# Grouped-query decode on one core: 8 MB tiles in three buffers, keys transposed in place, scores held in PSUM

## Chip, cores and metric

One core of a Trainium2 chip runs the kernel. The metric is device time in microseconds (us), the median of several executions. The engines are named as in the profile: PE (TensorE matmul), PEld (its weight load), DVE (VectorE), ACT (ScalarE), POOL (GpSimd) and SP (SyncE, which here only issues loads). "SPq" and "ACTq" are the queues from which SP and ACT issue DMAs; the transfers themselves run on 16 DMA engines.

## The reference

One query position attends to 65,536 keys. There are 32 query heads and 8 key/value heads, so four query heads share one key/value head (a group). All inputs are bf16.

```python
B, Hq, Hkv, Sq, Sk, D = 1, 32, 8, 1, 65536, 128
k = jnp.repeat(k, Hq // Hkv, axis=1)
v = jnp.repeat(v, Hq // Hkv, axis=1)
scores = jnp.einsum("bhqd,bhkd->bhqk", q, k) * D ** -0.5
p = softmax(scores, axis=-1)
return jnp.einsum("bhqk,bhkd->bhqd", p, v)
```

Keys and values are 134 MB each, and each is read once: 268.44 MB in all.

## The kernel before

A group's keys are laid out as 128 partitions of 512 rows (a row is 128 bf16 numbers, 256 B). They are loaded as four tiles of 128 rows a partition: 32 KB a partition, 4 MB a tile, one DMA each on SP's queue. Values are loaded in the same way. Keys and values share one pool of four such buffers (`iopool`, tag `io`).

The loop runs over g = 0 to 8 and s = 0 to 3. In each step it loads and uses key tile s of group g, and then value tile s of group g-1. So values run one group behind keys, and the last pass has values alone. Within that, a scheduler orders the instructions of an engine by their dependences; the loads on SP's queue go out in order, and each waits until its buffer is free.

A key tile goes through `k_step`. DVE transposes the tile, seen as 4-byte words, in 32x32 blocks into small buffers `T` (line 135, four instructions of 128x2048 words a tile). PE then multiplies each `T` with the group's queries, which lie spread out with zeros around them in `wq` (line 144, 32 matmuls of 512 columns a tile, all accumulating into one PSUM bank `sc`). ACT copies the bank to `S_g` in SBUF (line 151). There are two query buffers, `wq0` and `wq1`; POOL fills the one for the next group (line 109).

After four key tiles `softmax` takes the maximum over `S_g` (line 156), spreads the per-head maximum over the partitions with two small PE instructions (lines 160 and 172), and ends in `nmb` (line 174), the negated scaled maximum. ACT makes `E_g = exp(...)` in one instruction and sums it into `lsum_all` (line 177). `transpose_weights` transposes `E_g` into `ET` (line 190).

A value tile goes through `v_stream`: 32 matmuls with `ET` as weights (line 213), accumulating over the group into `psum_o`. `pick` takes the wanted blocks out of `psum_o` (lines 224 and 230), and `finish` divides by the sums and stores (lines 237 to 250). The last value tile is loaded in pieces of 64, 32, 16, 8, 4 and 4 rows, and `finish_last` treats its late rows one by one, so that little is left to do when the last piece lands.

At the start the queries come by four small transfers on ACT's queue (line 70), each a copy of all heads to 32 partitions, while SP already issues the first key loads.

Of the kernel before, what the change touches and what calls it, by code (L numbers as in the profile page):

```python
# [13 lines left out]
NT = 128  # L14
NW = 16
# [5 lines left out]
def kernel(  # L21
# [26 lines left out]
    W = NT // NW  # L48
    assert W * HPG == 32 and KT == 4
# [6 lines left out]
    iopool = ctx.enter_context(tc.tile_pool(name="iopool", bufs=4))  # L56
    tpool = ctx.enter_context(tc.tile_pool(name="tpool", bufs=3))
    spool = ctx.enter_context(tc.tile_pool(name="spool", bufs=2))
    epool = ctx.enter_context(tc.tile_pool(name="epool", bufs=2))
    opool = ctx.enter_context(tc.tile_pool(name="opool", bufs=2))  # L60
    stats = ctx.enter_context(tc.tile_pool(name="stats", bufs=2))
    psc = ctx.enter_context(tc.tile_pool(name="psc", bufs=3, space=bass.MemoryType.PSUM))
    psm = ctx.enter_context(tc.tile_pool(name="psm", bufs=1, space=bass.MemoryType.PSUM))
    psf = ctx.enter_context(tc.tile_pool(name="psf", bufs=1, space=bass.MemoryType.PSUM))
# [3 lines left out]
    qn = const.tile([P, D], bf16)  # L68
# [5 lines left out]
    Wq = []  # L74
    for x in range(2):
        wq = const.tile([P, 4 * WX], bf16, name=f"wq{x}")
        nc.vector.memset(wq[:, :], 0.0)
        Wq.append(wq)
# [17 lines left out]
    lsum_all = const.tile([P, Hkv], fp32)  # L96
    o_all = const.tile([P, Hkv, D], fp32)

# [5 lines left out]
    def queries(g):  # L104
        eng = nc.vector if g == 0 else nc.gpsimd
        wv = Wq[g % 2][:, :].rearrange("p (b r x) -> p b r x", b=2, r=2)
        for a in range(4):
            qd = slice(32 * a, 32 * a + 32)
            eng.tensor_copy(  # L109
                out=wv[qd, :, :, 32 * a + 28:32 * a + 28 + HPG],  # L110
                in_=qv[qd, :, :, g * HPG:(g + 1) * HPG],
            )
# [3 lines left out]
    S_tiles, E_tiles, ET_tiles, o_tiles = {}, {}, {}, {}  # L116

    def k_load(g, s):
        kn = iopool.tile([P, NT, D], bf16, name="kn", tag="io", align_bytes=2048)
        src = k[0, g].rearrange("(p n) d -> p n d", p=P)  # L120
        nc.sync.dma_start(out=kn[:, :, :], in_=src[:, s * NT:(s + 1) * NT, :])
        return kn

    def k_step(g, s, kn):
        if s == 0:
            S_tiles[g] = spool.tile([P, KT, 4 * P], fp32, name="S_g")
        wq = Wq[g % 2]
        kv = kn[:, :, :].rearrange("p (c w) d -> p w c d", w=W)
        sc = psc.tile([P, 4 * P], fp32, name="sc")
        for w in range(W):  # L130
            if s == 0 and w == W // 2 and g > 0:
                transpose_weights(g - 1)
            if w % 2 == 0:
                T = tpool.tile([P, 2, NW, D], bf16, name="T")
                nc.vector.transpose(  # L135
                    out=T[:, :, :, :].bitcast(fp32),
                    in_=kv[:, w:w + 2].bitcast(fp32),
                )
            Tv = T[:, w % 2].rearrange("p n (b i r) -> p n b i r", b=2, r=2)
            for b in range(2):  # L140
                for r in range(2):
                    bp = 2 * b + r
                    at = bp * WX + 28 - 4 * w
                    nc.tensor.matmul(  # L144
                        out=sc[:, :],
                        lhsT=wq[:, at:at + P],
                        rhs=Tv[:, :, b, :, r],
                        start=(w == 0 and bp == 0),
                        stop=(w == W - 1 and bp == 3),
                    )  # L150
        nc.scalar.copy(out=S_tiles[g][:, s, :], in_=sc[:, :])  # L151

    def softmax(g):
        S_g = S_tiles[g]
        mx = stats.tile([P, 1], fp32, name="mx")
        nc.vector.tensor_reduce(  # L156
            out=mx[:, :], in_=S_g[:, :, :].rearrange("p n c -> p (n c)"), axis=AX.X, op=ALU.max
        )
# [6 lines left out]
        mrow = stats.tile([1, P], fp32, name="mrow")  # L165
# [10 lines left out]
        E_g = epool.tile([P, KT, 4 * P], bf16, name="E_g")  # L176
        nc.scalar.activation(  # L177
            out=E_g[:, :, :].rearrange("p s x -> p (s x)"),
            in_=S_g[:, :, :].rearrange("p s x -> p (s x)"),
            func=ACT.Exp,  # L180
            bias=nmb[:, 0:1],
            scale=SCALE,
            accum_out=lsum_all[:, g:g + 1],
        )
        E_tiles[g] = E_g

    def transpose_weights(g):

        ET = epool.tile([P, KT, NW, 32], bf16, name="ET")
        nc.vector.transpose(  # L190
            out=ET[:, :, :, :].rearrange("p s c x -> p (s c x)"),
            in_=E_tiles[g][:, :, :].rearrange("p s x -> p (s x)"),
        )
        ET_tiles[g] = ET

    def v_load(g, s, pieces=(NT,)):
        vb = iopool.tile([P, NT, D], bf16, name="vb", tag="io", align_bytes=2048)
        src = v[0, g].rearrange("(p n) d -> p n d", p=P)
        x = 0
        for step in pieces:  # L200
            n0 = s * NT + x
            nc.sync.dma_start(out=vb[:, x:x + step, :], in_=src[:, n0:n0 + step, :])  # L202
            x += step
        return vb

    def v_stream(g, s, vb, rows, last):

        if s == 0:
            o_tiles[g] = pso.tile([P, 4, D], fp32, name="psum_o")
        for c in range(rows // W):  # L210
            for x in range(2):
                j = 2 * x + c % 2
                nc.tensor.matmul(  # L213
                    out=o_tiles[g][32 * j:32 * j + 32, :, :],
                    lhsT=ET_tiles[g][:, s, c, :],
                    rhs=vb[:, c * W + 4 * x:c * W + 4 * x + 4, :],
                    start=(s == 0 and c < 2),
                    stop=(last and c >= rows // W - 2),
                )

    def pick(g):

        o_m = opool.tile([P, 4, D], fp32, name="o_m")
        nc.vector.tensor_tensor(  # L224
            out=o_m[:, :, :],
            in0=o_tiles[g][:, :, :],
            in1=mask[:, :].unsqueeze(2).broadcast_to([P, 4, D]),
            op=ALU.mult,
        )
        nc.vector.tensor_reduce(  # L230
            out=o_all[:, g, :], in_=o_m[:, :, :].rearrange("p x d -> p d x"), axis=AX.X, op=ALU.add
        )

    def sums(g0, n):

        psum_l = psm.tile([HPG, n], fp32, name="psum_l", tag="misc")
        nc.tensor.matmul(out=psum_l[:, :], lhsT=sel[:, :], rhs=lsum_all[:, g0:g0 + n], start=True, stop=True)  # L237
        rl = stats.tile([HPG, n], fp32, name="rl")
        nc.vector.reciprocal(out=rl[:, :], in_=psum_l[:, :])
        return rl  # L240

    def store(g0, n, psum_f, rl):
        o_out = stats.tile([HPG, n, D], bf16, name="o_out")
        nc.vector.tensor_tensor(  # L244
            out=o_out[:, :, :],
# [3 lines left out]
        )  # L249
        nc.scalar.dma_start(  # L250
            out=out[0, :, 0, :].rearrange("(g h) d -> h g d", h=HPG)[:, g0:g0 + n, :], in_=o_out[:, :, :]
        )

    def finish(g0, n):
        rl = sums(g0, n)
        psum_f = psf.tile([HPG, n, D], fp32, name="psum_f", tag="fin")
        nc.tensor.matmul(  # L257
            out=psum_f[:, :, :], lhsT=sel[:, :], rhs=o_all[:, g0:g0 + n, :], start=True, stop=True
        )
        store(g0, n, psum_f, rl)  # L260

    def finish_last(g, s, vb):
# [6 lines left out]
        v_stream(g, s, vb, n1, True)  # L269
        pick(g)  # L270
        psum_oT = pso.tile([P, HPG], fp32, name="psum_oT", tag="psum_o")
        psum_f = psf.tile([HPG, 1, D], fp32, name="psum_f", tag="fin")

        def w4(n):
            c, w = divmod(n, W)
            return ET[:, s, c, HPG * w:HPG * w + HPG]

        def single(a, b):
            for n in range(a, b):
                nc.tensor.matmul(  # L280
                    out=psum_f[:, 0, :], lhsT=w4(n), rhs=vb[:, n, :], start=False, stop=(n == NT - 1)
                )

        with tc.manual_schedule(engines={mybir.EngineType.PE}):
            for n in range(n1, n2):
                if n == n1 + 32:
                    nc.tensor.matmul(  # L287
                        out=psum_f[:, 0, :], lhsT=sel[:, :], rhs=o_all[:, g, :], start=True, stop=False
                    )
                nc.tensor.matmul(  # L290
                    out=psum_oT[:, :], lhsT=vb[:, n, :], rhs=w4(n), start=(n == n1), stop=(n == n2 - 1)
# [4 lines left out]
            psum_t2 = psm.tile([HPG, D], fp32, name="psum_t2", tag="misc")  # L296
            nc.tensor.transpose(out=psum_t2[:, :], in_=oT[:, :], identity=ident[:, :])
            single(n3, NT)
        o_t = stats.tile([HPG, D], fp32, name="o_t")
        nc.vector.tensor_scalar_mul(out=o_t[:, :], in0=psum_t2[:, :], scalar1=rl[:, 0:1])  # L300
        o_last = stats.tile([HPG, D], bf16, name="o_last")
        nc.vector.scalar_tensor_tensor(  # L302
            out=o_last[:, :], in0=psum_f[:, 0, :], scalar=rl[:, 0:1], in1=o_t[:, :], op0=ALU.mult, op1=ALU.add
        )
        nc.scalar.dma_start(out=out[0, g * HPG:(g + 1) * HPG, 0, :], in_=o_last[:, :])

    for g in range(Hkv + 1):
        if 0 < g < Hkv:
            queries(g)
        for s in range(KT):  # L310
            if g < Hkv:
                k_step(g, s, k_load(g, s))
            elif s == 0:
                transpose_weights(g - 1)
# [44 lines left out]
```

## Time and profile before

| what | value |
|---|---|
| median of 3 runs | 632.07 us (631.75 to 632.32) |
| the profiled execution | 631.69 us |
| its span, first to last instruction | 629.6 us |
| granted TensorE clock, mean | 0.78 |
| busy: PE, DVE, ACT, POOL | 363.2, 340.4, 36.8, 6.4 us |
| loads on SP's queue | 69 DMAs, 268.44 MB |
| HBM rate over the span | 426 GB/s |
| SP's first load issued | 0.74 us after the span's start |

Times on the page are of one profiled execution, which is why its own time stands beside the span: 2.1 us lie outside the span. Busy time of an engine is a share of the whole span; whether it matters depends on what the others wait for. In the rows of groups, the numbers behind the bar are busy us, mean ns of one instruction, and the engine's idle time just before them with what ended it. In the rows of waits they are us in total, how many, and the longest.

### The profile page before, as it was taken

The page shows a single profiled execution, that of the slowest core. Times are in us where ns is not written, and L with a number is a line of the kernel's source. Part 1 is how long each engine was busy: PE and PEld are TensorE (multiplying, and loading weights), DVE is VectorE, ACT ScalarE, POOL GpSimd, SP SyncE. Part 2 cuts the span into 40 slices and gives each one's busy share as a digit, 9 for nine tenths or more (in the row PEclk, how much of TensorE's full clock was granted, in tenths as well). Part 3 has the DMA queues.
Part 4 walks back from the last instruction along what each step waited for, and adds up shares of the span by engine and source line. Part 5 has one row for each costly group of instructions (what it writes and reads, how often), then busy time and mean ns, then how long its engine had stood idle before and what let it go on. Part 6 is the DMA issues. An engine that isn't in the chain of part 4 may idle for free.

```text
span 629.6 us, 4872 instructions
## 1 busy us (share of the span) xinstructions
PE 363.2 (58%) x2133; PEld 141.5 (22%) x2133; DVE 340.4 (54%) x201; ACT 36.8 (6%) x49; POOL 6.4 (1%) x37
## 2 busy tenths in 40 slices
PE   0686836745557554575645856447665466644645
PEld 0232312211222221222211222112221122211212
DVE  0998833774337753377543775436754366553511
ACT  0000100010000100001000010001000010000100
POOL 0000000000000000000000000000000000000000
PEclk9998988767887677876778867788677787767856
DMA  8999999999999999999999999999999999999996
GB/s 369 433 434 431 433 432 434 432 433 433 432 433 432 433 433 432 433 432 433 432 433 433 430 434 434 433 432 433 435 432 433 432 433 433 432 433 434 431 430 267
DMA packets 10192, 268.78 MB, mean 427 GB/s; under 512 B 1340, under 2 KB 1596, under 8 KB 1852
## 3 DMA queue, kind: packets, MB, share of 16 engines
q1 hardware_dynamic: 9936, 268.44, 99.0%
q8 instruction: 16, 0.26, 0.1%
q10 hardware_dynamic: 236, 0.04, 0.0%
q14 instruction: 4, 0.03, 0.0%
HBM read 268.47 MB, written 0.01 MB: 426 GB/s over the span
## 4 chain that ended last, share of the span: by engine, by line
DMA 73%; DVE 12%; issue 11%; PE 2%; ACTq 0%; DVEq 0%; SPq 0%
DMA kn<-in_k_dram 66%; DVE T L135 12%; DMA vb<-in_v_dram 5%; DMA qn<-in_q_dram 2%; PE sc L144 2%; PE psum_o L213 0%; PE psum_oT L290 0%; ACTq L70 0%; PE psum_f L280 0%; DVEq L135 0%; DVE wq L109 0%; PE psum_f L287 0%; DVE sel L83 0%; DVE o_last L302 0%; SPq L202 0%
## 5 line engine op out<-in xcount | busy, mean ns | idle before, releaser
L144 PE MATMUL sc<-T,wq 128*128 128x512 bf16 x1024 | 287.9, 445 | 220.2 <-DVE T L135 220.2
L135 DVE STREAM_TRANSPOSE T<-kn 128x2048 f32<-128x2048 f32 x128 | 284.2, 2277 | 198.6 <-DMA kn<-in_k_dram 198.6
L144 PEld LDWEIGHTS <-wq 128*128 128x128 bf16 x1024 | 109.5, 109 | 394.6 <-issue 159.5
L213 PE MATMUL psum_o<-vb,ET 128*32 128x512 bf16 x1008 | 65.1, 403 | 12.0 <-DMA vb<-in_v_dram 9.8
L151 ACT COPY S_g<-sc 128x512 f32<-128x512 f32 x32 | 18.8, 587 | 510.8 <-PE sc L144 510.8
L213 PEld LDWEIGHTS <-ET 128*32 128x32 bf16 x1008 | 25.5, 100 | 49.2 <-issue 28.3
L156 DVE TENSOR_REDUCE mx<-S_g 128x1 f32<-128x2048 f32 x8 | 18.3, 2286 | 26.1 <-ACT S_g L151 26.1
L190 DVE STREAM_TRANSPOSE ET<-E_g 128x2048 bf16<-128x2048 bf16 x8 | 18.5, 2311 | 16.3 <-ACT E_g L177 16.3
L177 ACT ACTIVATE E_g<-S_g,nmb 128x2048 bf16<-128x2048 f32 x8 | 16.0, 2001 | 47.6 <-DVE nmb L174 40.4
L224 DVE TENSOR_TENSOR o_m<-psum_o,mask 128x512 f32<-128x512 f32 x8 | 5.5, 682 | 21.5 <-PE psum_o L213 21.5
L109 POOL COPY wq<-qx 32x16 bf16<-32x16 bf16 x28 | 5.3, 190 | 426.9 <-PE sc L144 410.2
L160 PE MATMUL psum_t<-ident,mx 128*1 128x128 f32 x8 | 2.2, 270 | 11.2 <-DVE mx L156 11.2
L100 DVE STREAM_TRANSPOSE qx<-qn 128x64 f32<-128x64 f32 x1 | 0.2, 245 | 15.0 <-DMA qn<-in_q_dram 15.0
L172 PE MATMUL psum_b<-one,mrow 1*128 1x1 f32 x16 | 3.5, 288 | 8.3 <-DVE mrow L166 8.3
L230 DVE TENSOR_REDUCE o_all<-o_m 128x128 f32<-128x512 f32 x8 | 8.0, 1000 | 0.0
L172 PEld LDWEIGHTS psum_b<-one,mrow 1*128 1x128 f32 x16 | 3.0, 232 | 12.2 <-issue 11.4
L237 PE MATMUL psum_l<-lsum_all,sel 128*4 128x4 f32 (+2 forms) x6 | 0.6, 166 | 7.7 <-ACT E_g L177 7.7
L257 PE MATMUL psum_f<-o_all,sel 128*4 128x512 f32 (+1 forms) x4 | 2.6, 730 | 2.9 <-DVE o_all L230 2.9
L160 PEld LDWEIGHTS psum_t<-ident,mx 128*1 128x1 f32 x8 | 0.6, 79 | 15.1 <-DVE mx L156 11.6
L174 DVE COPY nmb<-psum_b 128x1 f32<-128x1 f32 x8 | 1.2, 152 | 2.9 <-PE psum_b L172 2.9
L290 PE MATMUL psum_oT<-ET,vb 128*128 128x4 bf16 x56 | 1.8, 167 | 1.4 <-DMA vb<-in_v_dram 1.4
L244 DVE TENSOR_TENSOR o_out<-psum_f,rl 4x512 bf16<-4x512 f32 (+1 forms) x2 | 1.2, 612 | 2.5 <-PE psum_f L257 2.5
(30 smaller groups left out, 16.1 us busy)
## 6 DMA issues: line engine op xcount, KB each, us to landing
kn<-in_k_dram SPq DMA_DIRECT2D x32, 4096.0 KB, 29.6
vb<-in_v_dram SPq DMA_DIRECT2D x31, 4096.0 KB, 34.1
vb<-in_v_dram SPq DMA_DIRECT2D x1, 2048.0 KB, 29.5
vb<-in_v_dram SPq DMA_DIRECT2D x1, 1024.0 KB, 31.6
vb<-in_v_dram SPq DMA_DIRECT2D x1, 512.0 KB, 32.3
vb<-in_v_dram SPq DMA_DIRECT2D x1, 256.0 KB, 32.5
vb<-in_v_dram SPq DMA_DIRECT2D x2, 128.0 KB
qn<-in_q_dram ACTq DMA_DIRECT2D x4, 8.0 KB, 10.1
```

Of the source, the lines that this page charges most:

```text
L109: eng.tensor_copy(out=wv[qd, :, :, 32 * a + 28:32 * a + 28 + HPG], in_=qv[qd, :, :, g * HPG:(g + 1) * HPG],)
L135: nc.vector.transpose(out=T[:, :, :, :].bitcast(fp32), in_=kv[:, w:w + 2].bitcast(fp32),)
L144: nc.tensor.matmul(out=sc[:, :], lhsT=wq[:, at:at + P], rhs=Tv[:, :, b, :, r], start=(w == 0 and bp == 0), stop=(w == W - 1 and bp == 3),)
L151: nc.scalar.copy(out=S_tiles[g][:, s, :], in_=sc[:, :])
L156: nc.vector.tensor_reduce(out=mx[:, :], in_=S_g[:, :, :].rearrange("p n c -> p (n c)"), axis=AX.X, op=ALU.max)
L160: nc.tensor.transpose(out=psum_t[:, :], in_=mx[:, :], identity=ident[:, :])
L172: nc.tensor.matmul(out=psum_b[:, :], lhsT=mrow[:, :], rhs=one[:, :], start=True, stop=True)
L177: nc.scalar.activation(out=E_g[:, :, :].rearrange("p s x -> p (s x)"), in_=S_g[:, :, :].rearrange("p s x -> p (s x)"), func=ACT.Exp, bias= ...
L190: nc.vector.transpose(out=ET[:, :, :, :].rearrange("p s c x -> p (s c x)"), in_=E_tiles[g][:, :, :].rearrange("p s x -> p (s x)"),)
L213: nc.tensor.matmul(out=o_tiles[g][32 * j:32 * j + 32, :, :], lhsT=ET_tiles[g][:, s, c, :], rhs=vb[:, c * W + 4 * x:c * W + 4 * x + 4, :], ...
L224: nc.vector.tensor_tensor(out=o_m[:, :, :], in0=o_tiles[g][:, :, :], in1=mask[:, :].unsqueeze(2).broadcast_to([P, 4, D]), op=ALU.mult,)
L230: nc.vector.tensor_reduce(out=o_all[:, g, :], in_=o_m[:, :, :].rearrange("p x d -> p d x"), axis=AX.X, op=ALU.add)
```

## The change

- `NT` goes from 128 to 256 rows a partition: tiles are 64 KB a partition, 8 MB, two a group for keys and two for values. `iopool` has three buffers instead of four. A tile is worked through in halves of `NB` = 128 rows (`U` = 2 halves a tile, `NU` = 4 a group), and each half has its own PSUM bank `sc`.
- Keys are transposed in place: DVE writes the transposed words back over the tile, 128x4096 words an instruction, four a tile, and PE reads the tile itself. `T` goes. Which 16 rows go into one matmul changes with it: they are now next to each other.
- Scores stay in PSUM until the exp. The copy to `S_g` goes; DVE takes a maximum over each half's bank, and ACT makes four exps a group, one from each bank. There are five `sc` banks instead of three.
- `E_g`, `ET`, the query buffer `wq` and the statistics are single buffers. The query tile `qn` borrows the place of `E_g`. `ET` is made at the end of `softmax`.
- `pick` becomes four instructions that multiply and add, `finish` runs for two groups at a time, and results collect in `o_out`.
- Loads have one function, `load`. The first key tile comes in four pieces of 64 rows; the last value tile in pieces of 128, 64, 32, 16, 8, 4 and 4. Queries still come by four transfers.

```diff
-NT = 128
+NT = 256
+NB = 128
...
-    iopool = ctx.enter_context(tc.tile_pool(name="iopool", bufs=4))
-    tpool = ctx.enter_context(tc.tile_pool(name="tpool", bufs=3))
-    epool = ctx.enter_context(tc.tile_pool(name="epool", bufs=2))
-    psc = ctx.enter_context(tc.tile_pool(name="psc", bufs=3, space=bass.MemoryType.PSUM))
+    iopool = ctx.enter_context(tc.tile_pool(name="iopool", bufs=3))
+    epool = ctx.enter_context(tc.tile_pool(name="epool", bufs=1))
+    psc = ctx.enter_context(tc.tile_pool(name="psc", bufs=5, space=bass.MemoryType.PSUM))
...
+    def load(x, name, g, s, pieces=(NT,)):
+        t = iopool.tile([P, NT, D], bf16, name=name, tag="io", align_bytes=2048)
+        src = x[0, g].rearrange("(p n) d -> p n d", p=P)
+        n = 0
+        for step in pieces:
+            n0 = s * NT + n
+            nc.sync.dma_start(out=t[:, n:n + step, :], in_=src[:, n0:n0 + step, :])
+            n += step
+        return t
...
     def k_step(g, s, kn):
...
-            if w % 2 == 0:
-                T = tpool.tile([P, 2, NW, D], bf16, name="T")
-                nc.vector.transpose(
-                    out=T[:, :, :, :].bitcast(fp32),
-                    in_=kv[:, w:w + 2].bitcast(fp32),
-                )
...
-        nc.scalar.copy(out=S_tiles[g][:, s, :], in_=sc[:, :])
+        for u in range(U):
+            nu = s * U + u
+            sc = psc.tile([P, 4 * P], fp32, name="sc")
+            sc_tiles[g, nu] = sc
+            for w in range(W):
+                n0 = u * NB + w * NW
+                if w % 4 == 0:
+                    groups = kn[:, n0:n0 + 4 * NW, :].rearrange("p n d -> p (n d)").bitcast(fp32)
+                    nc.vector.transpose(out=groups, in_=groups)
+                kv = kn[:, n0:n0 + NW, :].rearrange("p n (b i r) -> p n b i r", b=2, r=2)
...
+            nc.vector.tensor_reduce(out=mx_tiles[g][:, nu:nu + 1], in_=sc[:, :], axis=AX.X, op=ALU.max)
...
+        for nu in range(NU):
+            nc.scalar.activation(
+                out=E_g[:, nu, :],
+                in_=sc_tiles[g, nu][:, :],
+                func=ACT.Exp,
+                bias=nmb[:, 0:1],
+                scale=SCALE,
+                accum_out=lsum_all[:, g, nu:nu + 1],
+            )
...
     def v_stream(g, s, vb, halves, last):
...
+        for u in range(U):
+            vv = vb[:, u * NB:(u + 1) * NB, :].rearrange("p (w c) d -> p w c d", c=NW)
+            n = min(2, halves - 2 * u)
+            for x in range(n):
+                for c in range(NW):
+                    j = 2 * x + c % 2
+                    nc.tensor.matmul(
+                        out=o_tiles[g][32 * j:32 * j + 32, :, :],
+                        lhsT=ET_tiles[g][:, s * U + u, c, :],
+                        rhs=vv[:, 4 * x:4 * x + 4, c, :],
...
     def pick(g):
...
+        nc.vector.tensor_scalar_mul(out=o, in0=o_tiles[g][:, 0, :], scalar1=mask[:, 0:1])
+        for x in range(1, 4):
+            nc.vector.scalar_tensor_tensor(
+                out=o, in0=o_tiles[g][:, x, :], scalar=mask[:, x:x + 1], in1=o, op0=ALU.mult, op1=ALU.add
+            )
...
-                k_step(g, s, k_load(g, s))
+                pieces = (64,) * 4 if g == 0 and s == 0 else (NT,)
+                k_step(g, s, load(k, "kn", g, s, pieces))
```

## The prediction

> **What bounds the kernel now.** I read the page's header and DMA rows first, then the queue's table, the groups by cost, the chain of waits, the waits of the SP queue and the timeline at both ends.
>
> ```profile
> span 629.6 us, 4872 instructions
> PE 363.2 (58%) x2133; PEld 141.5 (22%) x2133; DVE 340.4 (54%) x201; ACT 36.8 (6%) x49; POOL 6.4 (1%) x37
> ...
> DMA  8999999999999999999999999999999999999996
> GB/s 369 433 434 431 433 432 434 432 433 433 432 433 432 433 433 432 433 432 433 432 433 433 430 434 434 433 432 433 435 432 433 432 433 433 432 433 434 431 430 267
> ...
> q1 hardware_dynamic: 9936, 268.44, 99.0%
> ```
>
> No compute engine is above 58%, while the one queue that carries keys and values fills 99.0% of what 16 engines have, at 430 to 435 GB/s in every slice but the first and the last. There is no dip at a group's end or anywhere else, so nothing that the compute engines do holds a load up. The packet records of the trace say the same: the first data packet starts at 1.75 us, the last ends at 625.51 us, and all packets of q1 last together 623.24 us an engine. Of the 623.76 us between them the engines lack 0.5 us. So the span is 1.75 us, then the loads, then 4.1 us of tail.
>
> ```profile
> SPq L121 <- DVE T L135: 273.7, 28, 14.2
> ...
> SPq L202 <- PE psum_o L213: 108.4, 28, 5.0
> ```
>
> SP does wait for buffers: a key buffer comes free when DVE has transposed it out, a value buffer when PE has read it. These waits cost nothing, because a load lands 29.6 us (keys) or 34.1 us (values) after its issue, which is three transfers of 9.7 us: two are still queued ahead at the issue. The chain of waits has the same shape all along:
>
> ```profile
> 72.41 2.07 issue
> 74.62 2.06 issue
> 76.67 4.47 DVE T L135 x2
> 81.16 29.74 DMA kn<-in_k_dram
> ```
>
> Its DMA pieces are three transfers long, so a third of each is time spent behind other loads. I take from it only who frees the buffer.
>
> **What a packet costs.** The packet records (median ns) are 46 for 1,024 B, 84 for 2,048, 159 for 4,096, 309 for 8,192, 611 for 16,384, and 1,213 for 32,768, of which there are 8,064; a 4-byte completion write takes 9 and there are 1,104. These lie on one line: from 16,384 to 32,768 B it is 602 ns, so 32,768 B cost 1,204 ns of bytes and about 9 ns that belong to the packet. One engine's sum before: 504 packets of 1,213, 8 x (611+309+159+84+46+46) for the last tile's pieces, 69 completions of 9, together 622.0 us. The trace's 623.24 has 1.2 us more; about 0.6 us of that is the first packets at 1.4 to 2.0 us instead of 1.2.
>
> **Part 1, tiles of 8 MB.** A row becomes 65,536 B. Not in this trace. Extended from the pair 16 KB and 32 KB it costs 2,417 ns, from 1 and 32 KB 2,418, from 8 and 32 KB 2,418; if the row goes out as two packets, 2 x 1,213 = 2,426. I take 2,417, since all pairs agree on the line, and keep 2,426 for the upper end. One engine after:
> - first tile in four pieces: 32 packets of 611 = 19.55 us
> - 30 whole tiles: 240 packets of 2,417 = 580.08 us
> - last tile: 8 x 1,213, then the six short pieces as before = 19.74 us
> - 41 completions of 9 = 0.37 us
>
> The sum is 619.74 us against 622.01, a gain of **2.27 us**: 240 packet costs of 9 ns (2.16 us) and 28 completions (0.25 us) saved, 0.14 us lost in the first tile.
>
> A rule to weigh here: the Trainium skill (DMA: Bandwidth & Descriptors, section on the anatomy of one DMA) fits a GpSimd-issued transfer as 2.0 us plus its bytes at 436 GB/s. Taken as a cost for each of 28 transfers removed, that rule would make the gain 56 us, an estimate from its figure. The row above contradicts it for queued transfers: the engines' idle time over all 69 transfers is 0.5 us.
>
> **Part 2, three buffers in place of four, keys released by PE.** This is the part that could cost time. A pair of tiles takes 2 x (8 x 2,417 + 9) ns = 38.7 us to load. When a key tile lands, the two other buffers hold 38.7 us of loads at most, and the refill needs about 1 us from issue to first packet (0.74 to 1.75 us at the start). So a key tile must be consumed within 37.6 us of landing.
>
> ```profile
> L144 PE MATMUL sc<-T,wq 128*128 128x512 bf16 x1024 | 287.9, 445 | 220.2 <-DVE T L135 220.2
> ...
> L135 DVE STREAM_TRANSPOSE T<-kn 128x2048 f32<-128x2048 f32 x128 | 284.2, 2277 | 198.6 <-DMA kn<-in_k_dram 198.6
> ```
>
> Transposes: 64 of 128x4096 replace 128 of 128x2048, four a tile. Twice 2,277 is 4.55 us; four of the old run back to back in 8.89 us, which gives 4.45. In place is not in the trace; I take 4.5, so 18 us a tile. PE follows with 16 matmuls each: the last tile's start 0.43 us apart at 580 to 585 us (granted clock 0.5) and later about half that, so the last 16 add 3.4 to 6.8 us. A key tile is done 21.4 to 24.8 us after landing. With every matmul at the slow clock it is 4.5 + 64 x 0.427 = 31.8 us. Cover left: 12.8 us, at worst 5.8.
>
> A value tile is 64 matmuls, 3.8 to 7.2 us (32 take 1.91 or 3.61 us now). PE's order stays key, value, key, value, so a value tile that lands 19.35 us after its key tile starts when PE is done at 24.8 and ends at 32.0, far ahead of its own limit of 57. The in-order queues agree: SP issues four pieces, two key tiles, then values and keys in turn, and no load stands behind one that lands later.
>
> A rule that speaks against it: the Trainium skill (TensorE: Matmul & The Clock Gate, section on HAM oscillation) says that a wait for a DMA between tiles sends the clock back to half. The trace shows that already, at 0.5 after such waits. The 31.8 us above was worked out from rows for that case.
>
> **Part 3, scores in PSUM until the exp; single E, ET and query buffers.** ACT's 32 copies (587 ns) go; DVE takes 32 maxima of 128x512 from PSUM, by the nearest row (the L224 product, 682 ns) 0.7 us each, in place of 8 of 2.29 us. The new waits stand at a group's end. DVE holds the ET transpose (and behind it the next tile's first transposes) until PE has read ET for the last value tile, at 32.0 us after the last key tile's landing; then come the four picks (1 us), the chain to nmb (2.6), four exps at 0.59 + 0.19 (3.1) and ET (2.3): 41 us, 2.3 us after the next key tile landed. POOL's four query copies (0.93 us at 278.56) now wait for the group's last matmul, and PE for them; they lie inside the same time. A fifth PSUM bank holds the next half tile meanwhile. These 2.3 us come out of the 12.8 us of cover: nothing on the path. Without cover they would cost 2.3 us in each of 7 groups, 16 us.
>
> **Part 4, both ends.** Queries go out as the same four transfers, interleaved packet for packet with the keys: they land at 16.5 us now because each of 12 rounds waits for a 1.2 us packet. Beside 16 KB packets a round is 0.63 us, so about 10 us. The first tile is then done near 30 us; its buffer is wanted at 1.75 + 58.6 = 60. No gain, no loss. The tail keeps its six small pieces and its last matmuls; four picks of about 0.25 us for 0.69 + 1.03 us end before the last load. Zero.
>
> **Sum.** The profiled execution took 631.69 us (span 629.6 and 2.1 around it), so 629.4 after. It lies 0.38 us below the median of three, 632.07; on that basis **629.8 us**. Runs scattered from 631.75 to 632.32.
>
> **The rivals.**
> - *No gain, 631.96 us:* the 64 KB row is sent as two packets. Then 28 completions less and 16 packets more leave 0.11 us. For it: no packet above 32,768 B is in the trace. Against it: every row so far, from 1 to 32 KB, went out as one packet.
> - *Slower:* reading and writing the same buffer makes the transpose slow enough that the three buffers run dry. It decides at 4x + 4.5 = 37.6, x = 8.3 us for one 128x4096 transpose. At twice my value, 9.0 us, a key tile takes 40.5 us of the 37.6 it has: 2.9 us for each of 16 key tiles, 46 us, so about 676 us. For it: the operation is unseen and the buffers are fewer. Against it: one read and one write an element, as now, and DVE is idle for 46% of the span.
>
> **How the numbers follow.** Forecast 0.80, two packets 0.09, slower by whatever stall 0.11. The forecast's own range is 629.3 to 630.4: scatter of 0.3 us and 0.3 us for the two ends of the kernel. The whole range goes up to the rival without gain and its scatter: 629.3 to 632.2. This leaves out the slow rival and little else. What can be told from no change is 0.2%, 1.3 us: faster below 630.8.
>
> **What would show it.** Right: packets of 65,536 B with a median near 2,417 ns; 5,904 q1 packets in place of 9,936 (252 fewer an engine); first and last packet 2.3 us closer; no slice below 430 GB/s between the ends; loads landing about 35 us (values, into a key buffer) and 45 us (keys) after issue; transposes near 4.5 us; queries landed by about 10 us. Wrong: 32,768 B packets as the main size; a slice below 425 GB/s; a DMA gap at a group's end, with SP's waits for PE's matmuls longer than 37 us; or packets longer than 2,426 ns.

## The result and the profile after

The changed kernel took 629.61 us (median of 10, 629.43 to 631.48) beside 631.86 us for the kernel before on the same chip: a ratio of 0.9969, interval 0.9960 to 0.9979. Forecast were 629.8 us and a range of 629.3 to 632.2. On another chip the same kernel took 631.28 us (629.76 to 635.93) beside 631.90: 0.9991, interval 0.9977 to 1.0005. So the total came out as forecast the first time and cannot be told from no change the second. Both are explained below; the sum behind the forecast had a term that was too large, and two terms that it put at nothing, the tail and the time outside the span, moved.

The page of the changed kernel, its header, its DMA rows and its queue:

```profile
span 627.7 us, 4762 instructions
PE 346.2 (55%) x2141; PEld 145.4 (23%) x2141; DVE 339.2 (54%) x193; ACT 23.6 (4%) x65; POOL 6.4 (1%) x37
...
DMA  9999999999999999999999999999999999999996
GB/s 369 435 468 402 464 405 460 409 456 413 452 418 448 422 443 427 439 430 435 434 431 439 431 435 434 431 439 427 443 426 444 422 448 418 448 418 452 410 423 281
...
q1 hardware_dynamic: 5904, 268.44, 99.0%
```

The load queue still fills 99.0%, now with 5,904 packets, as forecast: the 64 KB row goes out as one packet (3,840 of 65,536 B, median 2,418 ns; forecast 2,417). The GB/s row now swings between 402 and 468, which the prediction had named as a sign of error. It is not one. The packets of the 16 engines run nearly in step; 16 of them are 1.05 MB, or 67 GB/s of a slice of 15.7 us, and the row counts each packet whole in the slice in which it starts. Neighbouring slices average 435, and with the same buffers and compute but packets of 32 KB (the first experiment) the row is flat at 431 to 434.

Groups, waits of the SP queue and load issues of the changed kernel:

```profile
L141 PE MATMUL sc<-kn,wq 128*128 128x512 bf16 x1024 | 260.1, 415 | 242.9 <-DVE kn L135 242.6
L135 DVE STREAM_TRANSPOSE kn<-kn 128x4096 f32<-128x4096 f32 x64 | 279.0, 4414 | 149.2 <-DMA kn<-in_k_dram 149.2
...
L148 DVE TENSOR_REDUCE mx<-sc 128x1 f32<-128x512 f32 x32 | 21.5, 673 | 53.0 <-PE sc L141 53.0
```
```profile
SPq L120 <- DVE kn L135: 431.5, 16, 31.5
SPq L120 <- PE psum_o L197: 61.7, 13, 8.0
SPq L120 <- PE sc L141: 59.0, 16, 3.8
```
```profile
kn<-in_k_dram SPq DMA_DIRECT2D x15, 51.6
vb<-in_v_dram SPq DMA_DIRECT2D x15, 36.7
```

The transpose in place takes 4,414 ns, no more than two of the old. The maximum takes 673 ns (0.7 forecast). Value loads, which go into a key buffer, land 36.7 us after issue (35 forecast), key loads 51.6 us (45 forecast; the value tile was read in 4.5 us where I had reckoned 7.2, after a key tile that was done sooner). The longest wait of the queue for PE is 8.0 us, where more than 37 would have been a sign of a stall, and between 30 and 610 us the DMA engines are idle for less than 0.06 us on average in any 4 us.

Where the time went, from the packet records and the last instruction of each profiled execution:

| us | before | changed | changed, second profile |
|---|---|---|---|
| first packet to last | 623.76 | 622.48 | 623.12 |
| last packet to end of span | 4.06 | 3.42 | 5.00 |
| outside the span | 2.12 | 1.87 | 1.78 |

From the first packet to the last the loads gave 1.3 us, not 2.27; in the second profile 0.6. The tail, for which I had put zero, is 0.6 us shorter in one profile and 0.9 longer in the other.

### The profile page after: what moved, and what is told of

Same layout as the page of the kernel before. It is cut to its first block, busy times and chain, and to the rows that moved or that the text cites. A ratio compares the mean times of both kernels' runs of the same rounds, so it can differ in the third digit from the quotient of the medians.

```text
span 627.7 us, 4762 instructions
## 1 busy us (share of the span) xinstructions
PE 346.2 (55%) x2141; PEld 145.4 (23%) x2141; DVE 339.2 (54%) x193; ACT 23.6 (4%) x65; POOL 6.4 (1%) x37
## 3 DMA queue, kind: packets, MB, share of 16 engines
q1 hardware_dynamic: 5904, 268.44, 99.0%
## 4 chain that ended last, share of the span: by engine, by line
DMA 41%; DVE 23%; PE 23%; another core or an unknown queue 11%; ACT 1%; issue 1%; SPq 0%; DVEq 0%; ACTq 0%
DMA kn<-in_k_dram 35%; DVE kn L135 20%; PE sc L141 17%; DMA vb<-in_v_dram 5%; PE psum_o L197 5%; ACT E_g L172 1%; DMA qn<-in_q_dram 1%; DVE o_pair L215 1%; DVE mx L148 1%; DVE ET L181 0%; PE psum_b L166 0%; PE psum_f L234 0%; DVE m L156 0%; PE psum_t L154 0%
## 5 line engine op out<-in xcount | busy, mean ns | idle before, releaser
L141 PE MATMUL sc<-kn,wq 128*128 128x512 bf16 x1024 | 260.1, 415 | 242.9 <-DVE kn L135 242.6
L135 DVE STREAM_TRANSPOSE kn<-kn 128x4096 f32<-128x4096 f32 x64 | 279.0, 4414 | 149.2 <-DMA kn<-in_k_dram 149.2
L141 PEld LDWEIGHTS <-wq 128*128 128x128 bf16 x1024 | 104.9, 103 | 395.9 <-issue 173.2
L197 PE MATMUL psum_o<-vb,ET 128*32 128x512 bf16 x1008 | 76.6, 394 | 11.1 <-DMA vb<-in_v_dram 11.1
L148 DVE TENSOR_REDUCE mx<-sc 128x1 f32<-128x512 f32 x32 | 21.5, 673 | 53.0 <-PE sc L141 53.0
L197 PEld LDWEIGHTS <-ET 128*32 128x32 bf16 x1008 | 34.7, 99 | 50.4 <-issue 19.1
L172 ACT ACTIVATE E_g<-sc,nmb 128x512 bf16<-128x512 f32 x32 | 21.6, 686 | 564.4 <-DVE nmb L168 564.4
L213 DVE TENSOR_SCALAR o_pair<-psum_o,mask 128x128 f32<-128x128 f32 x8 | 2.8, 350 | 49.2 <-PE psum_o L197 49.2
L215 DVE SCALAR_TENSOR_TENSOR o_pair<-psum_o,mask,o_pair 128x128 f32<-128x128 f32 x24 | 8.3, 345 | 0.5
L172 ACT ACTIVATION_READ_ACCUMULATOR E_g<-sc,nmb 128x1 f32 x32 | 6.5, 203 | 0.0
(31 smaller groups left out, 15.7 us busy)
## 6 DMA issues: line engine op xcount, KB each, us to landing
kn<-in_k_dram SPq DMA_DIRECT2D x15, 51.6
```

The costliest lines, as they stand in the source:

```text
L135: nc.vector.transpose(out=groups, in_=groups)
L141: nc.tensor.matmul(out=sc[:, :], lhsT=wq[:, at:at + P], rhs=kv[:, :, b, :, r], start=(w == 0 and bp == 0), stop=(w == W - 1 and bp == 3),)
L148: nc.vector.tensor_reduce(out=mx_tiles[g][:, nu:nu + 1], in_=sc[:, :], axis=AX.X, op=ALU.max)
L172: nc.scalar.activation(out=E_g[:, nu, :], in_=sc_tiles[g, nu][:, :], func=ACT.Exp, bias=nmb[:, 0:1], scale=SCALE, accum_out=lsum_all[:, g, ...
L197: nc.tensor.matmul(out=o_tiles[g][32 * j:32 * j + 32, :, :], lhsT=ET_tiles[g][:, s * U + u, c, :], rhs=vv[:, 4 * x:4 * x + 4, c, :], start ...
L213: nc.vector.tensor_scalar_mul(out=o, in0=o_tiles[g][:, 0, :], scalar1=mask[:, 0:1])
```

## The experiments

Each kernel ran beside the kernel before on its chip; the ratio is to that. The letters stand for the theories of the expectations: by A a packet costs its recorded duration, by A' the distance from its start to the next one's, and by B the gain does not come from packets at all.

**1. Two DMAs a tile.**

```diff
-pieces = (64,) * 4 if g == 0 and s == 0 else (NT,)
+pieces = (64,) * 4 if g == 0 and s == 0 else (128, 128)     # values alike
```

> The changed kernel, but each whole 8 MB load goes out as two DMAs of 128 rows a partition: buffers, order and compute stay, packets are 32 KB again. Theory A (my sum: a packet costs 9 ns beyond its bytes, by the recorded durations): 30 tiles x (16 x 1,213 + 2 x 9 - 8 x 2,418 - 9 ns) = 2.2 us more, 631.8 us. Theory A' (packets overlap in the records, and the start-to-start time counts: 19,318 ns for an 8 MB tile against 2 x 9,681 for two of 4 MB): 30 x 44 ns = 1.3 us more, 630.9 us. Rival B (the gain comes from the compute side, the start or the tail, not from packets): 629.6 us as the changed kernel, with the last packet as early as there.

Measured: 631.05 us, ratio 0.9987 (0.9978 to 0.9996). From the first packet to the last it takes 623.9 us: 1.4 more than in the changed kernel (0.8 more than in its second profile), and as long as in the kernel before. That is nearer to A' (1.3) than to A (2.2), and B falls. The time alone would not settle it, since the ratio lies between the two of the changed kernel, 0.9969 and 0.9991. What is left of the gain lies behind the last packet (tail 3.6 us) and outside the span (1.8 us).

**2. Four DMAs a tile.** `(64,) * 4` for every tile.

> The changed kernel, but each whole 8 MB load goes out as four DMAs of 64 rows a partition, packets of 16 KB. Theory A: 30 x (32 x 611 + 4 x 9 - 19,353 ns) = 7.1 us more, 636.7 us. Theory A': with 4 ns of overlap a packet the pitch is 607 ns and a completion 6 ns, 30 x (32 x 607 + 24 - 19,318 ns) = 3.9 us more, 633.5 us. Rival B: 629.6 us.

Measured: 633.71 us, ratio 1.0035 (1.0021 to 1.0050). A' had 633.5, A 636.7. From the first packet to the last it takes 626.4 us, 3.9 more than in the changed kernel, where A' had 3.9 and A 7.1. Its header and queue row show why A is too dear:

```profile
span 631.8 us, 4867 instructions
...
q1 hardware_dynamic: 18864, 268.44, 99.4%
```

99.4% of 631.8 us is 628.0 us of recorded packets an engine, in those 626.4 us. More packet time than time: the records overlap. What counts is the distance from one start to the next on an engine (the records name no engine; a packet is put behind the one that has just ended). It is 1,209 ns for a 32 KB packet (recorded as 1,213) and 2,414 for 64 KB (2,418), so one of 64 KB saves 4 to 5 ns over two of 32 KB, and not 9; a tile of 8 MB starts 19,318 ns after the one before, two of 4 MB 19,362.

**3. The first key tile in one DMA.** `pieces = (NT,)` for all key tiles.

> The changed kernel with the first key tile as one DMA of 64 KB packets instead of four pieces. All theories on the path: the DMA engines gain 0.1 to 0.2 us, 629.4 to 629.6 us, nothing to be told from the changed kernel. The queries, 12 packet rounds of 2.41 us, land at about 31 us instead of 10.8, and the first tile is done by about 31 + 22 = 53 us, before its buffer is wanted at 60. Rival: the start has less cover than I worked out and the late queries cost a stall of the loads, over 631 us, with a slice below 400 GB/s before 100 us.

Measured: 633.80 us, ratio 1.0034 (1.0021 to 1.0046). Slower than the kernel before. The rival was right. By stretches, with the share of DMA and the GB/s last in the row:

```profile
90.00:95.00 5.00, 4.31 (x21) 1.75 (x20) 5.00 (x3) 0.00 (x0) 0.00 (x0) 1.00 1.06 459
95.00:100.00 5.00, 3.73 (x18) 1.60 (x17) 2.23 (x1) 0.00 (x0) 0.00 (x0) 1.00 0.52 223
100.00:105.00 5.00, 5.00 (x67) 2.30 (x66) 4.04 (x2) 0.00 (x0) 0.00 (x0) 1.00 0.65 226
```

The DMA engines are idle near 100 us, for 2.6 us on average. The SP queue's timeline shows what they waited for, here and then in the changed kernel:

```profile
100.95 0.33 SPq L120 DMA_DIRECT2D vb<-in_v_dram  x1
```
```profile
89.79 0.33 SPq L120 DMA_DIRECT2D vb<-in_v_dram  x1
```

At the start three key tiles follow each other without values between them. Each takes 21 us to work through and 19.3 to load, so a late start is never made up, and the third has the score maximum, the exps and the ET transpose of the first group in its way. Its buffer takes the second value load. With the tile in pieces that load is issued 11.2 us before the load ahead of it has landed; with the late queries (29.7 us) it goes out 11.2 us later, and 0.1 us is left.

**4. The changed pick alone, in the kernel before.**

```diff
-nc.vector.tensor_tensor(out=o_m, in0=o_tiles[g], in1=mask..., op=ALU.mult)
-nc.vector.tensor_reduce(out=o_all[:, g, :], in_=o_m..., axis=AX.X, op=ALU.add)
+nc.vector.tensor_scalar_mul(out=o, in0=o_tiles[g][:, 0, :], scalar1=mask[:, 0:1])
+for x in range(1, 4):
+    nc.vector.scalar_tensor_tensor(out=o, in0=o_tiles[g][:, x, :], scalar=mask[:, x:x + 1], in1=o, ...)
```

> The kernel before with the changed pick alone (four multiply-adds in place of a product and a reduction). My sum: no change, 631.9 us, 4.1 us from the last packet to the end of the span, since the pick ends before the last load lands. Rival B, in part: the changed pick shortens the tail, 3.5 us from the last packet to the end and 631.3 us. If the tail is set by the granted clock in the last 10 us instead, its length goes with the clock there and not with the pick.

Measured: 631.85 us, ratio 0.9998 (0.9990 to 1.0007), tail 4.2 us. No change, as my sum had it.

**5 and 6. More DVE work a key unit.** A maximum over part of the raw tile goes ahead of each transpose.

```diff
+extra = stats.tile([P, 1], fp32, name="extra")
+nc.vector.tensor_reduce(out=extra[:, :], in_=groups[:, :2048], axis=AX.X, op=ALU.max)   # or 3072
 nc.vector.transpose(out=groups, in_=groups)
```

> The changed kernel with a DVE maximum over 128x2048 of the raw tile, its result unused, before each in-place transpose: 2.29 us by the row of the kernel before, so that a unit of DVE work is x = 4.41 + 2.29 = 6.7 us instead of 4.41. My rule for a buffer (4x + 4.5 below 37.6 us): 31.3 us, no stall, 629.6 us. A rule for a whole group (DVE and the chain at a group's end in series, 2 x (4x + 4.3) + 10.4 us against the 77.3 us that a group loads in): 72.6 us, no stall either. If the cover is smaller than both say, over 635 us.

> The same with a maximum over 128x3072, about 3.35 us, x = 7.8 us. My rule for a buffer, threshold 8.3 us: 4 x 7.8 + 4.5 = 35.7 us, below 37.6, no stall, 629.6 us. The rule for a group: 2 x (4 x 7.8 + 4.3) + 10.4 = 81.4 us against 77.3, DVE-bound, 4.1 us for each of 8 groups, 33 us more, about 662 us; if the scheduler interleaves the chain with the next tile's transposes, less of it, down to none.

Measured: 642.30 us (ratio 1.0163, 1.0130 to 1.0196) and 677.08 us (1.0713, 1.0682 to 1.0744). Neither rule had a stall in the first; the cover was smaller than both said. In the second mine had no stall either, and the rule for a group, with 662 us, fell 15 us short. The extra instructions took 2.26 and 3.32 us, as reckoned. In the first run the DMA engines are idle for 6.2 us on average near 100 us:

```profile
90.00:100.00 10.00, 5.24 (x22) 2.06 (x21) 9.96 (x6) 2.79 (x8) 0.00 (x0) 0.96 0.74 321
100.00:105.00 5.00, 5.00 (x21) 1.85 (x21) 1.86 (x2) 0.00 (x0) 0.00 (x0) 0.75 0.00 0
```

and 0.6 to 1.4 us again near 260, 415 and 575 us. The load near 100 us went out 3.6 us after the load ahead had landed. The three others, which had 1.0, 1.8 and 1.7 us in hand, lost 1.4, 0.6 and 0.9, so a refill needs about 2.5 us of lead on that landing, where I had reckoned 1.0. The 1.0 us was right for what it named: the first packet follows the issue by 0.96 us each time. But a load lands when the last of the 16 engines is done, and on average they finish 1.2 to 1.3 us before that and then have nothing left to do. Between x = 4.41 and 6.67 us the lead near 90 us falls from 11.2 to -3.6 us; on a straight line it meets 2.5 at x = 5.7, an estimate from these two runs.

**7. Two buffers.** `bufs=2` in `iopool`.

> The changed kernel with two buffers of 8 MB instead of three. A key tile holds its buffer for 4 x 4.41 + 3.65 = 21.3 us after landing, to which 1 us from issue to first packet comes; the other buffer holds 19.3 us of loads. So each key tile costs a gap of about 3 us: 16 x 3 = 48 us, about 678 us, and more where a group's end delays a key tile (up to 10 us for 7 groups, 748 us). Rival: the loads do not depend on when a key tile is consumed, as the even rate of before would suggest: 629.6 us.

Measured: 701.96 us, ratio 1.1107 (1.1075 to 1.1139). The rival falls. There are 15 gaps of 62 us in sum, mostly 3.5 to 5 us each, more than the 3 us reckoned with the short lead. On top, the packets of the run sum to 10.3 us more an engine than in the changed kernel: a load after a gap has about 20.0 us of packets an engine, any other 19.35. The first packets of the kernel before are longer too, 1.4 to 2.0 us against 1.2.

**8. The changed kernel again.**

> The changed kernel a second time, for a second profile and for times beside the two kernels sent with it. Theory A' (packets give 1.2 to 1.3 us, the rest lies behind the last packet and outside the span): last packet at 624.2 us, tail about 3.5 us with the granted clock at 1.0 when the last packet lands, 1.8 us outside the span, 629.6 us. If the short tail was an accident of one profile: tail 4.1 us.

Measured: 631.28 us, ratio 0.9991 (0.9977 to 1.0005); last packet at 624.85, tail 5.0 us, which neither forecast had. Timelines of the tail, first profile and then this one, each with a row by stretches in which the granted clock stands third from the end:

```profile
619.60:621.40 1.80, 1.80 (x16) 0.77 (x15) 0.00 (x0) 0.00 (x0) 0.00 (x0) 1.00 1.00 402
```
```profile
619.57 1.90 PE L197 MATMUL psum_o<-vb,ET 128*32 128x512 bf16 x16 [2.06 <-DMA vb<-in_v_dram]
...
625.64 0.27 ACTq L296 DMA_DIRECT2D out_dram<-o_out  x1
```
```profile
620.30:623.60 3.30, 3.30 (x16) 1.08 (x15) 0.00 (x0) 0.00 (x0) 0.00 (x0) 0.50 0.71 280
```
```profile
620.21 3.59 PE L197 MATMUL psum_o<-vb,ET 128*32 128x512 bf16 x16 [2.08 <-DMA vb<-in_v_dram]
...
625.40 0.38 PE L275 MATMUL psum_f<-o_pair,sel 128*4 128x128 f32 x2 [0.72 <-DVE o_pair L215]
...
627.85 0.27 ACTq L296 DMA_DIRECT2D out_dram<-o_out  x1
```

The same 16 matmuls, on the last piece of 64 rows, take 1.90 us at a granted clock of 1.0 and 3.59 at 0.5. In the second profile the clock fell at 620.24 us, after 2.08 us in which PE had nothing to do. The idle time alone does not decide it, for it was as long in the first profile (2.06 us), where the clock stayed. In every profile here the granted clock holds for whole multiples of 3.41 us (but for the last stretch), and where these steps lie differs between executions. In the second profile one was at 620.24 us; in the first, counted on from the change at 609.25, they were at 619.49 and 622.90. That this decides between the two lengths is likely and not shown. Whether the chip matters is open too: the three profiles from this one (experiments 8 to 10) have tails of 5.0 to 5.3 us, the variants profiled on others (1 to 3 and 5 to 7) 3.4 to 4.0.

The pick follows the 16 matmuls, and a PE instruction that needs the pick (line 275) stands in PE's hand-written order ahead of the last rows' matmuls. In the kernel before the same piece takes 1.05 us at a clock of 1.0 (1.90 in the fourth experiment, where it was at 0.5):

```profile
620.85 1.05 PE L213 MATMUL psum_o<-vb,ET 128*32 128x512 bf16 x16 [1.46 <-DMA vb<-in_v_dram]
```

Its 16 matmuls write four column groups of PE (32 of its 128 columns each) in turn, while in the changed kernel this piece is one half x of the loop and writes two. The records of the single matmuls agree: in the kernel before four start within 25 ns, in the changed one two, and in both the next ones start about 216 ns after these at a clock of 1.0.

**9. The value loops swapped.** `for c` outside, `for x` inside, as before.

> The changed kernel with the two inner loops of the value matmuls swapped back to the order of before (blocks of 16 rows outside, halves inside), so that neighbouring matmuls write four column groups of PE in turn instead of two. Loads: no change, last packet at 624.2 us. Theory C (the tail is shorter because the value matmuls of the changed kernel take longer, 64 in 4.5 us against 32 in 1.91, and keep the clock up): value matmuls fall back to 60 ns apart, the clock is at 0.5 when the last packet lands and the tail is 4.1 us, 630.2 us. Rival: the order has nothing to do with the tail, 3.5 us and 629.6 us.

Measured: 630.37 us, ratio 0.9982 (0.9973 to 0.9991), runs from 629.9 to 632.1, tail 5.0 us in the profile. Inconclusive as a test of the tail: the last piece has one x only, so its 16 matmuls keep two column groups in either order and took 3.60 us. But on a whole value tile the order does what the column groups let one expect. Here 64 matmuls, four groups in turn, and then the changed kernel, both at a clock of 1.0:

```profile
161.52 3.64 PE L197 MATMUL psum_o<-vb,ET 128*32 128x512 bf16 x64
```
```profile
161.06 4.55 PE L197 MATMUL psum_o<-vb,ET 128*32 128x512 bf16 x64
```

**10. The first tile whole, queries ahead of it.**

```diff
-nc.scalar.dma_start(out=qn[32 * a:32 * a + 32, :], in_=q[0, :, 0, :])
+nc.sync.dma_start(out=qn[32 * a:32 * a + 32, :], in_=q[0, :, 0, :])     # and pieces = (NT,)
```

> The changed kernel with the first key tile as one DMA, and the four query transfers moved to SP's queue ahead of the keys. They delay the first key packet by four issues, about 2 us. Theory D (late queries cost the 4.2 us of the run with the whole first tile, because three key tiles follow each other at the start and each lags the loads): queries land by about 4 us, DVE starts on the first tile when it lands at about 23 us, no gap near 100 us, 629.6 + 2 - 0.1 = 631.5 us. Rival (the whole first tile costs it by itself, since DVE starts at 23 us and not at 12): the gap near 100 us stays and the time is about 635.7 us.

Measured: 633.27 us, ratio 1.0014 (1.0006 to 1.0023), runs from 631.7 to 633.7. By stretches:

```profile
90.00:95.00 5.00, 4.95 (x36) 2.15 (x39) 0.69 (x1) 0.00 (x0) 0.00 (x0) 1.00 0.97 419
95.00:100.00 5.00, 3.18 (x52) 1.39 (x44) 0.00 (x0) 0.00 (x0) 0.00 (x0) 1.00 0.99 423
100.00:105.00 5.00, 0.00 (x0) 0.00 (x0) 1.86 (x1) 0.00 (x0) 0.00 (x0) 0.82 0.97 419
```

The gap is gone, with the first tile still whole: the late queries cost it, not the whole tile. The last packet ends at 626.24 us, 1.4 to 2.0 later than in the changed kernel, as the four issues ahead of the keys have it. The time is still 1.8 us above the 631.5 of theory D: the profile has a tail of 5.3 us, of the kind of experiment 8, where D reckoned with a short one. So the time lies between D and its rival, and the missing gap is what decides.

**11 and 12. PE kept busy near the end,** in the changed kernel and in the kernel before.

```diff
+def warm(t, n):
+    ps = psc.tile([P, 4 * P], fp32, name="sc")
+    for x in range(n):
+        nc.tensor.matmul(out=ps[:, :], lhsT=t[:, 0, :], rhs=t[:, 0:4, :], start=(x == 0), stop=(x == n - 1))
```

> The changed kernel with 16 more matmuls on PE whose results nobody reads: 8 after the last but one value tile and 8 between the first and the second piece of the last tile, where PE is idle. Theory C' (the tail has two lengths, 3.4 us with the clock at 1.0 and 5.0 with 0.5 when the last piece of 64 rows lands, because its 16 matmuls write two column groups only and take 1.9 or 3.6 us): the clock stays at 1.0 up to the last packet, the 16 matmuls take 1.9 us, tail 3.4 us in every run, 629.6 us with a scatter of a few tenths. Rival (the long tail has another cause): 631.3 us and the scatter of the changed kernel.

> The kernel before with such matmuls: 16 after value tile 1 and 8 after value tile 2 of the last group. Theory C': the clock is at 1.0 when the last packet lands; the tail goes from 4.1 to about 3.6 us, since only the small matmuls and the pick's start get shorter, 631.4 us. Against the changed kernel with the same matmuls this leaves what the loads give: A' 1.2 to 1.3 us (last packet at 625.5 against 624.2), and 0.3 us outside the span. Rival: 632.0 us.

Both kernels also put the value matmuls of the last tile into PE's hand-written order, so that the added ones stay where they are meant to be.

Measured: the changed kernel 629.61 us in runs from 629.42 to 629.94, ratio 0.9960 (0.9948 to 0.9973); the kernel before 631.50 us, ratio 0.9988 (0.9979 to 0.9997). The timeline of the first:

```profile
617.92 1.90 PE L190 MATMUL sc<-vb 128*128 128x512 bf16 x8
620.05 1.90 PE L204 MATMUL psum_o<-vb,ET 128*32 128x512 bf16 x16 [0.23 <-DMA vb<-in_v_dram]
```

The clock stays at 1.0, the 16 matmuls take 1.90 us and the tail 3.45. The scatter of the changed kernel, 1.9 us in experiment 8 without its one outlier, is 0.5 us here. That fits C', but five runs are few: the changed kernel did not run on this chip, and on the first one seven of its ten runs also lay between 629.4 and 629.8 us. So the steadier time is likely and not shown. Of all that ran, this kernel has the lowest ratio to the kernel before. In the kernel before the median fell by 0.6 us as C' had it, but the profiled tail did not (4.09 us; the clock fell 0.5 us before the last packet), so there C' is not shown. Beside each other on this chip the two profiles differ by 1.88 us: 1.13 from the first packet to the last (622.89 and 624.02), 0.64 in the tail and 0.11 outside the span.

## Why the prediction was right or wrong

**What bounds the kernel: right.** The loads do; the time from the first packet to the last follows the packets in experiments 1 and 2, and a queue that runs dry costs time (experiments 3 and 5 to 7).

**What a packet costs: the line right, the size wrong.** A 64 KB packet is on the line. But I took recorded durations for cost, and 9 ns beyond the bytes in each. Starts are 4 ns closer than that, a completion costs 6 ns and not 9. With 44 ns a tile (19,362 less 19,318), 30 tiles give 1.3 us, and the pieces of the first tile take back under 0.1. The term of 2.27 us measures 1.2 to 1.3 by starts, and 0.6 to 1.3 from first to last packet, where the uneven ends of 16 engines come in (1.1 between experiments 11 and 12). The trace of before already had it: a 32 KB packet there starts 1,209 ns after the one ahead of it and is recorded as 1,213.

The prediction also weighed 2.0 us for each transfer, the fixed part that the Trainium skill (DMA: Bandwidth & Descriptors, section on the anatomy of one DMA) gives for a transfer issued by GpSimd. It does not carry over to transfers queued one behind the other: 28 fewer brought nowhere near 56 us.

**Part 2, the buffers: no stall, right; the cover and its threshold wrong.** I looked at one key tile in the steady state, 17 us of lead there by the issues, and did not follow three in a row at the start, where it is 11.2. With the lead of 2.5 us that a refill needs here, the slow rival decides near x = 5.7 us (the estimate of experiment 5) and not at 8.3. The transpose took 4.41, so it did not decide.

**Part 3: right.** The single buffers and the scores in PSUM cost nothing on the path: the DMA engines of the changed kernel show no gap at any group's end, and with packets of 32 KB again it is not slower than the one before (experiment 1).

**Part 4: the start right in its outcome and not in its reason, the tail wrong.** The queries landed at 10.4 us and the start cost nothing, as forecast. But the buffer of the first tile was not the one to look at. With the queries at 29.7 us (experiment 3) that buffer was still free in time, 8.3 us before the load ahead landed; the one of the third tile was not, and the change was slower than the kernel before. So the four pieces, put at "no gain, no loss", carry the result. "Zero" for the tail: it moved by -0.6 or +0.9 us with the clock, and the changed kernel feels the clock more than the one before, since its last value piece uses two column groups.

So the forecast of 2.27 us was met the first time by 1.3 us from packets, 0.6 from a tail in its short form and some 0.3 outside the span. That the three add up to it is luck: with the tail in its long form, as on the second chip, most of the gain is gone. The last term is no accident of a profile. Time less span is 1.75 to 1.84 us on average in the changed kernel and each of its variants, and 1.97 to 2.16 in the kernel before and its two, over all runs; what causes it is open, and it was not tried.

**The rivals.** Two packets for a row: excluded by the packet records. A stall: did not happen, but was nearer than a chance of 0.11 and a price of 46 us suggest: one stall of 2.6 us was enough to make the change slower than the kernel before (experiment 3).

## What to carry to other kernels

When one queue of loads is full, read the cost of a packet from start to start on an engine, not from its recorded duration, and test it by cutting the packets: a fit over sizes can be perfect and still count overlap. Work out the cover of buffers for the start and for each change of phase, tile by tile, with the lead that a refill needs, and not only for the steady state. A tail of small matmuls after the last load inherits the clock that PE had while it waited: count how many column groups the last piece uses, and where the clock decides, try keeping PE busy.

## What the runs showed of the hardware

- A small transfer on one queue waits for one packet of the other queue at each of its rounds: beside key packets of 32, 16 and 64 KB the rounds of the queries start about 1.22, 0.61 and 2.43 us apart. Queries of 256 B rows landed at 16.1, 10.4 and 29.7 us.
- Recorded packets of one engine overlap by about 4 ns, so that their sum can exceed the elapsed time (628.0 us of packets in 626.4 us).
- To keep the queue full, a load had to be issued about 2.5 us before the one ahead of it landed: 0.96 us to its first packet, and most of the rest because the 16 engines are done 1.2 to 1.3 us before that landing on average.
- A queue that ran dry pays more than the gap: in the run with two buffers, packets took 10.3 us more an engine in all, with 15 gaps.
- Value matmuls of 32 columns by 512 take 1.05 us for 16 in four column groups and 1.90 in two at a granted clock of 1.0; at 0.5 they take 1.90 and 3.59.
